# Chunk 3's transposes moved from the crossbar to TensorE, and batch 0's sink rows of v moved up in Pool's queue

## The chip, the cores and the metric

The kernel runs on one core of one Trainium2 chip. Times are device microseconds (us) of an execution; lower is better. The kernel before takes 211.6 us in the median of 6 runs (211.2 to 212.99). The engines are named as in the profile: PE (TensorE, with PEld for its weight loads), DVE (VectorE), ACT (ScalarE), POOL (GpSimd), SP (SyncE, which here only issues transfers).

## What is computed

Attention with a sliding window and four sink positions, followed by a feed-forward layer that takes the maximum of three products:

```python
batch, n_heads, seq, head_dim = (4, 8, 768, 64);  n_sink, window = (4, 128)
n_tokens, d_model, d_ff = (3072, 512, 768)

scores = scale * q @ k.T
keep   = (pos_k < n_sink) | ((0 <= pos_q - pos_k) & (pos_q - pos_k < window))
a      = softmax(where(keep, scores, -1e9))
x      = (a @ v), heads side by side                    # 3072 x 512
h      = maximum(maximum(x @ w1, x @ w2), x @ w3)       # 3072 x 768
out    = h @ w_out                                      # 3072 x 512, float32
```

Inputs and output are float32; products run in bfloat16 with float32 sums.

## The kernel before

The 3072 tokens are cut into 12 chunks of 256, three for each of the four batches. A chunk passes through these steps, each a letter in the order that is written out by hand:

- load (L61): K and Q in halves of four heads (`qk_raw`, four transfers), V in four transfers (`v_raw`), all issued by SP. A gate may be given: a one-element memset on Pool that the load has to wait for.
- cast (L186): to bfloat16, `cast_qk` (L172) four times into `qk_bf` and `cast_v` (L182) twice into `ve`. For chunks 0 and 1 VectorE and Pool share it; from chunk 2 on Pool does it. The layout of `qk_bf` differs by how it will be transposed: by half heads for TensorE, or in one run for the crossbar.
- K and Q (`prep`, L200): four PE transposes each for half the heads into a PSUM tile `pt`; K is then copied by VectorE (two copies, `place_k`, L192) into `kz`, Q by ScalarE (L209) into `qT`. From chunk 2 on `pt` comes from the pool `ps_o`, which has two buffers and also serves the steps A and T.
- D and E: the other way to the same end. `turn` (L215) issues two crossbar transposes on SP, of K to `kT` and of Q straight to `qT`; E (`place_k` from `kT`) copies K with two larger VectorE copies.
- S (`score`, L233): scores of one head, the exponential on ScalarE (L249) and, for each pair of heads, the mask on VectorE (L252).
- Z: sink scores of a chunk (L254), or, for the first chunk of a batch, the gathering of the batch's sink rows of K (`sink_k`, L223).
- A (`av`, L268): products with V for four heads and half the tokens. Chunks other than a batch's first begin with the sink product (L272), which reads `vs`. L280 are the window's products, the first of each head with the earlier block of 128 rows. L285 and L288 normalize.
- T: transposes of the result on PE (L300) and a copy by ScalarE (L301).
- F (L306): one of nine products with w1, w2, w3, taken up by ScalarE (L317) or VectorE (L319). Y (L321): the product with w_out, the copy to `y_sb` (L329), and the stores on SP (L336), issued after the second half.

Work is issued in the order of the program text, and each engine runs its own instructions strictly in that order. Chunks 0, 1 and 2 have an order of their own (L371 to L440), in which small "warm" products fill PE; from L442 on a loop runs ten passes, pass i with the scores and A of chunk i+1, F and Y of chunk i, D and E of chunk i+2 and the load and cast of chunk i+3.

`sink_v(b)` (L163) spreads the four sink rows of V of batch b over the heads: one Pool multiplication (L164) of `vs_raw` with a 0/1 mask `bm`, and a small copy (L168). `vs_raw` holds the sink rows of all batches; SP loads it with four small transfers (L89) between the loads of chunks 0 and 1.

Two places matter for the change. In the opening (L381 to L394) Pool runs: two casts of v of chunk 0, half of chunk 1's K and Q casts, the issue of w1, the other half, the issues of the second and third weights, the gate of load 2, two casts of v of chunk 1, `sink_v(0)`, and zeros for `kz[2]`. And where the opening hands over to the loop (L436 to L440) SP gets, in this order, the stores of chunk 0's output (Y of chunk 0 is in the line before), the two crossbar transposes of chunk 3, load 4, and the stores of chunk 1's output.

Of the kernel before, what the change touches and what calls it, by code (L numbers as in the profile page):

```python
# [16 lines left out]
def kernel(  # L17
# [24 lines left out]
    CPB = S // 256  # L42
# [8 lines left out]
    with tc.manual_schedule():  # L51
# [9 lines left out]
        def load(ci, gate=None):  # L61

            b, c = divmod(ci, CPB)
            t0 = c * 256
            eng = nc.sync
            qk = raw.tile([128, 2, 2, 512], F32, tag="qk_raw", name="qk_raw")
            vr = raw.tile([128, 2, H, D], F32, tag="v_raw", name="v_raw")
            if gate is not None:
                gate.memset(qk[0:1, 0, 0, 0:1], 0.0)
            for g in range(2):  # L70
                for j, src in ((0, k), (1, q)):
                    eng.dma_start(  # L72
                        out=qk[:, j, g].rearrange("p (h i d) -> p h (i d)", h=4, d=D),
                        in_=src[b, 4 * g:4 * g + 4, t0:t0 + 256]
                            .rearrange("h (p i) d -> p h (i d)", i=2))
            for n in range(2):
                for i in range(2):
                    eng.dma_start(  # L78
                        out=vr[64 * i:64 * i + 64, n],
                        in_=v[b, :, t0 + 128 * n:t0 + 128 * n + 128]  # L80
                            .rearrange("h (p i) d -> i p h d", i=2)[i])
            raws[ci] = (qk, vr)
# [17 lines left out]
        def zeros(i, c, eng):  # L100
            for h in range(2):
                eng.memset(kz[CPB * i + c][64 - 64 * h:128 - 64 * h, h], 0.0)
# [37 lines left out]
        def load_w(wi):  # L140
            w = (moe_w1, moe_w2, moe_w3)[wi]
            wt = const.tile([128, DS, d_ff], BF16, name=f"w{wi}")
            nc.gpsimd.dma_start(out=wt, in_=w.rearrange("(a p) f -> p a f", p=128))
            w_sb[wi] = wt
# [18 lines left out]
        def sink_v(b):  # L163
            nc.gpsimd.tensor_tensor(  # L164
                out=vs[0:R, b, :, 0:D],
                in0=vs_raw[:, b].unsqueeze(1).to_broadcast([R, H, D]),
                in1=bm.unsqueeze(2).to_broadcast([R, H, D]), op=ALU.mult)
            nc.gpsimd.tensor_copy(vs[0:R, b, :, D:D + 1], bm.unsqueeze(2))  # L168
# [3 lines left out]
        def cast_qk(ci, j, g, eng):  # L172
            if ci not in bfs:
                bfs[ci] = raw.tile([128, 2, 2, 2, 256], BF16, tag="qk_bf", name="qk_bf")
            src = raws[ci][0][:, j, g].rearrange("p (h i d) -> p h i d", h=4, d=D)
            if ci < CPB:
                dst = bfs[ci][:, j, g]
            else:
                dst = bfs[ci][:, j].rearrange("p i a x -> p i (a x)")[:, :, 256 * g:256 * g + 256]
            eng.tensor_copy(dst.rearrange("p i (h d) -> p h i d", d=D), src)  # L180

        def cast_v(ci, n, eng):  # L182
            b, c = divmod(ci, CPB)
            eng.tensor_copy(ve[b % 2][:, 2 * c + n, :, 0:D], raws[ci][1][:, n])  # L184

        def cast(ci):  # L186
            for j, g in ((0, 0), (1, 0), (0, 1), (1, 1)):
                cast_qk(ci, j, g, nc.gpsimd)
            for n in range(2):
                cast_v(ci, n, nc.gpsimd)  # L190
# [147 lines left out]
        def step(op):  # L338

            name, ci, arg = op[0], int(op[1:3]), op[3:]  # L340
            if ci >= NCH:
                return
            if name in "KQ":
                prep(ci, int(name == "Q"), int(arg))
            elif name == "D":
                turn(ci)
            elif name == "E":
                place_k(ci, kTs.pop(ci), slice(0, NP))
            elif name == "S":
                score(ci, int(arg))  # L350
            elif name == "Z":
                if ci % CPB:
                    sink_score(ci)
                elif ci > 0:
                    sink_k(ci // CPB)
            elif name == "A":
                av(ci, int(arg[0]), int(arg[1]))
            elif name == "T":
                xpose(ci, int(arg))
            elif name == "F":  # L360
                ffn_h(ci, int(arg))
            elif name == "Y":
                ffn_y(ci, int(arg))

        def run(text, **at):
            for tok in text.split():
                c = at[tok[1]]
                step(f"{tok[0]}{c:02d}{tok[2:]}")


        sink_v_init()  # L371
        warm(36)
        cast_qk(0, 0, 0, nc.vector)
        cast_qk(0, 1, 0, nc.vector)
        run("Ka0", a=0)
        warm(4)
# [6 lines left out]
        cast_qk(1, 0, 0, nc.gpsimd)  # L383
        cast_qk(1, 1, 0, nc.gpsimd)
        load_w(0)
        cast_qk(1, 0, 1, nc.gpsimd)
        cast_qk(1, 1, 1, nc.gpsimd)
        load_w(1)
# [1 line left out]
        load(2, nc.gpsimd)  # L390
        cast_v(1, 0, nc.gpsimd)
        cast_v(1, 1, nc.gpsimd)
        sink_v(0)
        zeros(0, 2, nc.gpsimd)  # L394
        run("Sa0 Sa1 Ka1", a=0)
        warm(3)
# [37 lines left out]
        for b in range(1, B):  # L434
            sink_v(b)
        run("Sc3 Sc4 Fb5 Ac00 Sc5 Fb8 Ac01 Sc6 Ya0 Sc7 Ya1", a=0, b=1, c=2)  # L436
        run("Dd", d=3)
        load(4)
        cast(4)
        run("Ac10 Ac11 Yb0 Tc0 Tc1 Yb1 Ed", b=1, c=2, d=3)  # L440

        for i in range(2, NCH):  # L442
            run("Dc", c=i + 2)
# [43 lines left out]
```

## Time and profile before

| | |
|---|---|
| median of 6 runs | 211.6 us |
| the profiled execution | 211.76 us |
| its span, first to last instruction | 210.1 us |
| mean granted PE clock | 0.966 |
| busy: PE, DVE, ACT, POOL | 186.0, 121.2, 107.5, 67.0 us |
| share of the 16 DMA engines taken by SP's queue | 63.5% |

In the slices each digit is the busy share in tenths, over a fortieth of the span. The granted clock is the share of its full speed that PE had. In the chain of waits each step leads back to what released it; in the list by time a line gives start, length, and engine with tile and line. A wait is put down to the instruction that came last before the waiting one could go.

### The profile page before, as it was taken

To read this page: it belongs to the slowest core of one execution; us is meant where nothing else is said; L and a number is where in the kernel's file an instruction comes from. 1 tells how busy PE (TensorE), PEld (TensorE's weight loads), DVE (VectorE), ACT (ScalarE), POOL (GpSimd) and SP (SyncE) were. 2 spreads that over 40 slices of the span, in tenths; PEclk is the share of its full clock that TensorE was granted. 3 is DMA by queue.
4 is the path that set the end of the run, shared out by engine and by line. 5 is a ranking of instruction groups with operands and counts; after the bars stand their busy time and mean duration, and the time that the engine had idled before them with its cause. 6 is when DMAs were issued, how large, how long until landed. Compare 5 with 4: busy or idle time off the path is not lost.

```text
span 210.1 us, 4734 instructions
## 1 busy us (share of the span) xinstructions
PE 186.0 (89%) x1895; PEld 149.1 (71%) x1895; DVE 121.2 (58%) x271; ACT 107.5 (51%) x198; POOL 67.0 (32%) x113
## 2 busy tenths in 40 slices
PE   7765187999929999999999999999999999999991
PEld 7644176887507959969869689599697797796860
DVE  4792042589413875755748837846668477375340
ACT  8865055145433638456465466375472853754321
POOL 7364448997003335340250420701602400000000
PEclk9997579999996999999999999999999999999999
DMA  5999995960199899959939969869579680300304
GB/s 153 230 220 199 214 264 112 258 166 0 38 187 262 172 261 212 256 123 175 265 72 167 295 129 197 208 116 250 139 151 260 135 158 3 87 16 0 100 3 100
DMA packets 75749, 33.37 MB, mean 159 GB/s; under 512 B 45776, under 2 KB 72656, under 8 KB 75728
## 3 DMA queue, kind: packets, MB, share of 16 engines
q1 hardware_dynamic: 73344, 29.93, 63.5%
q0 software_dynamic: 2384, 3.15, 9.0%
q8 instruction: 15, 0.25, 0.5%
q14 instruction: 6, 0.05, 0.1%
HBM read 25.20 MB, written 6.29 MB: 150 GB/s over the span
## 4 chain that ended last, share of the span: by engine, by line
PE 63%; DVE 13%; DMA 8%; SPq 6%; ACT 4%; issue 3%; POOL 1%; DVEq 0%; POOLq 0%
PE h_ps L313 40%; PE y_ps L324 8%; DMA v_raw<-in_v_dram 6%; DVE h_sb L319 5%; PE st L242 4%; DVE x_sb L288 4%; PE o_ps L280 4%; DMA kT<-qk_bf 3%; SPq L78 2%; DVE e_sb L252 2%; ACT e_sb L249 2%; PE st L243 2%; PE xt_ps L300 2%; SPq L72 2%; PE st L240 1%
## 5 line engine op out<-in xcount | busy, mean ns | idle before, releaser
L313 PE MATMUL h_ps<-xT,w 128*128 128x256 bf16 x864 | 109.5, 275 | 0.7 <-ACT xT L301 0.7
L313 PEld LDWEIGHTS <-w 128*128 128x128 bf16 x864 | 82.0, 99 | 10.7 <-issue 0.8
L249 ACT ACTIVATE e_sb<-st 128x512 bf16<-128x512 f32 (+1 forms) x96 | 53.4, 564 | 35.5 <-PE st L243 35.4
L319 DVE TENSOR_TENSOR h_sb<-h_sb,h_ps 128x512 bf16<-128x512 bf16 x72 | 49.2, 684 | 21.4 <-PE h_ps L313 18.9
L180 POOL CAST qk_bf<-qk_raw 128x512 bf16<-128x512 f32 x44 | 29.2, 673 | 85.1 <-DMA qk_raw<-in_k_dram 69.5
L252 DVE TENSOR_TENSOR e_sb<-e_sb,msk 128x1024 bf16<-128x1024 bf16 (+1 forms) x48 | 32.4, 675 | 41.2 <-ACT e_sb L249 41.0
L324 PE MATMUL y_ps<-wo,h_sb 128*128 128x512 bf16 x144 | 35.2, 379 | 0.0
L329 ACT COPY y_sb<-y_ps 128x512 f32<-128x512 f32 x24 | 14.1, 586 | 37.1 <-PE y_ps L324 37.1
L242 PE MATMUL st<-qT,kz 128*128 128x256 bf16 x96 | 26.5, 280 | 5.3 <-DVE kz L196 4.3
L317 ACT CAST h_sb<-h_ps 128x512 bf16<-128x512 f32 x36 | 21.1, 586 | 15.1 <-PE h_ps L313 14.9
L280 PEld LDWEIGHTS <-e_sb 128*128 128x128 bf16 x352 | 17.1, 99 | 8.6 <-issue 5.5
L243 PE MATMUL st<-qT,kz 128*128 128x128 bf16 x96 | 21.4, 224 | 0.0
L288 DVE TENSOR_TENSOR x_sb<-o_ps,rc 128x256 bf16<-128x256 f32 x48 | 20.4, 425 | 1.7
L324 PEld LDWEIGHTS <-h_sb 128*128 128x128 bf16 x144 | 12.4, 98 | 12.5 <-DVE h_sb L319 3.2
L280 PE MATMUL o_ps<-ve,e_sb 128*128 128x65 bf16 x352 | 19.1, 196 | 1.3 <-DVE e_sb L252 1.3
L184 POOL CAST ve<-v_raw 128x512 bf16<-128x512 f32 x24 | 15.7, 662 | 13.0 <-DMA v_raw<-in_v_dram 12.6
L242 PEld LDWEIGHTS <-kz 128*128 128x128 bf16 x96 | 9.5, 99 | 6.8 <-issue 4.5
L240 PE MATMUL st<-qT,kz 128*128 128x128 bf16 x64 | 14.2, 223 | 0.0
L272 PE MATMUL o_ps<-vs,e_sink 128*128 128x260 bf16 x32 | 9.0, 282 | 5.3 <-POOL vs L168 5.3
L301 ACT COPY xT<-xt_ps 128x512 bf16<-128x512 bf16 x24 | 13.2, 595 | 0.7 <-PE xt_ps L300 0.7
L285 DVE RECIPROCAL rc<-o_ps 128x4 f32<-128x4 f32 x48 | 8.4, 176 | 8.4 <-PE o_ps L280 8.4
L196 DVE COPY kz<-kT 64x1024 bf16<-64x1024 bf16 x18 | 9.2, 514 | 5.9 <-DMA kT<-qk_bf 5.6
(44 smaller groups left out, 110.6 us busy)
## 6 DMA issues: line engine op xcount, KB each, us to landing
qk_raw<-in_k_dram SPq DMA_DIRECT2D x24, 256.0 KB, 4.5
qk_raw<-in_q_dram SPq DMA_DIRECT2D x24, 256.0 KB, 5.4
v_raw<-in_v_dram SPq DMA_DIRECT2D x48, 128.0 KB, 4.2
out_dram<-y_sb SPq DMA_DIRECT2D x22, 256.0 KB, 4.3
w<-in_moe_w_dram POOLq DMA_DIRECT2D x3, 768.0 KB, 9.6
wo<-in_moe_w_out_dram POOLq DMA_DIRECT2D x2, 384.0 KB, 5.6
out_dram<-y_sb SPq DMA_DIRECT2D x4, 128.0 KB, 2.3
kT<-qk_bf SPq DMA_TRANSPOSE x9, 5.0
```

The lines of the kernel that those rows point to most:

```text
L180: eng.tensor_copy(dst.rearrange("p i (h d) -> p h i d", d=D), src)
L240: nc.tensor.matmul(st[:, 0], lhsT=kz[(ci - 1) % (2 * CPB)][:, h, p, 128:256], rhs=qh[:, 0], start=True, stop=True)
L242: nc.tensor.matmul(st[:, 1:3], lhsT=kh[:, 0:128], rhs=qh, start=True, stop=True)
L243: nc.tensor.matmul(st[:, 3], lhsT=kh[:, 128:256], rhs=qh[:, 1], start=True, stop=True)
L249: nc.scalar.activation(e[:, h, lo:], st[:, lo:], AF.Exp, scale=scale)
L252: nc.vector.tensor_tensor(out=e[:, :, lo:], in0=e[:, :, lo:], in1=m, op=ALU.mult)
L280: nc.tensor.matmul(o[:, hh], lhsT=es[ci, p][:, h, sl], rhs=ve[b % 2][:, n, 2 * p + h], start=(c == 0 and x == 0), stop=(x == len(blocks) - 1),
L288: nc.vector.tensor_mul(xs[ci, t][:, 4 * g:4 * g + 4], o[:, :, 0:D], rc.unsqueeze(2).to_broadcast([128, 4, D]))
L313: nc.tensor.matmul(hp[:, f], lhsT=w_sb[wi][:, ds, (2 * fp + f) * 128:(2 * fp + f + 1) * 128], rhs=xTs[ci][:, ds, :], start=(ds == 0), stop ...
L317: nc.scalar.copy(dst, hp)
L319: nc.vector.tensor_max(dst, dst, hp)
L324: nc.tensor.matmul(yp, lhsT=hs[ci][:, fb, t * 128:(t + 1) * 128], rhs=wo[:, fb], start=(fb == 0), stop=(fb == FB - 1))
```

## The change

1. Chunk 3 is transposed by PE (K and Q steps), and the crossbar is used from chunk 4 on. `cast_qk` lays chunk 3 out by half heads accordingly. The four `prep` steps stand between the last steps of chunk 2's A, chunk 1's Y and chunk 2's T; D and E of chunk 3 go.
2. `sink_v(0)` goes from behind the v casts of chunk 1 to behind the issue of the first weights, ahead of the second half of chunk 1's K and Q casts.

```diff
@@ cast_qk
-            if ci < CPB:
+            if ci <= CPB:
                 dst = bfs[ci][:, j, g]
             else:
                 dst = bfs[ci][:, j].rearrange("p i a x -> p i (a x)")[:, :, 256 * g:256 * g + 256]
@@ the opening
         cast_qk(1, 0, 0, nc.gpsimd)
         cast_qk(1, 1, 0, nc.gpsimd)
         load_w(0)
+        sink_v(0)
         cast_qk(1, 0, 1, nc.gpsimd)
         cast_qk(1, 1, 1, nc.gpsimd)
         load_w(1)
         load_w(2)
         load(2, nc.gpsimd)
         cast_v(1, 0, nc.gpsimd)
         cast_v(1, 1, nc.gpsimd)
-        sink_v(0)
         zeros(0, 2, nc.gpsimd)
@@ before the loop
         run("Sc3 Sc4 Fb5 Ac00 Sc5 Fb8 Ac01 Sc6 Ya0 Sc7 Ya1", a=0, b=1, c=2)
-        run("Dd", d=3)
         load(4)
         cast(4)
-        run("Ac10 Ac11 Yb0 Tc0 Tc1 Yb1 Ed", b=1, c=2, d=3)
+        run("Ac10 Ac11 Yb0 Tc0 Kd0 Tc1 Qd0 Yb1 Kd1 Qd1", b=1, c=2, d=3)
```

In the text of the order a token is the step's letter, a letter for the chunk, and the step's part: "Kd0" is K of chunk d = 3, first half of the heads.

## The prediction

> **What bounds the kernel now.** I read the 40 slices first, to find stages where TensorE (PE) is not busy; then the waits of PE; then the chain of waits through the two holes; then the busy time by stretches, which gives the clock; last the timeline of each engine around the holes.
>
> The slices, from the page (each is 5.25 us):
>
> ```profile
> PE   7765187999929999999999999999999999999991
> PEclk9997579999996999999999999999999999999999
> ```
>
> From the thirteenth slice on (63 us) PE is full to the end, so nothing after that can be won except by starting it earlier. Two holes lie before: slice five (21 to 26 us) and slice twelve (58 to 63 us), each followed by a low granted clock. The waits put names to them:
>
> ```profile
> PE o_ps L272 <- POOL vs L168: 5.3, 1, 5.3
> PE st L242 <- DVE kz L196: 4.3, 1, 4.3
> ```
>
> The chain, in order of time (start, length, what):
>
> ```profile
> 12.05 11.64 DMA v_raw<-in_v_dram
> ...
> 24.39 1.04 POOL vs L164
> 25.43 0.18 POOL vs L168
> 25.61 0.04 issue
> 25.65 0.38 PE o_ps L272
> ...
> 54.90 0.59 ACT y_sb L329
> ...
> 56.20 0.62 SPq L336
> ...
> 56.91 5.44 DMA kT<-qk_bf
> 62.35 0.02 issue
> 62.38 0.42 DVE kz L196
> 62.83 0.44 DVE kz L196
> 63.26 0.36 PE st L242
> ```
>
> First hole: PE waits for the sink rows, which Pool writes only after the cast of v of chunk 1, whose data land at 23.7. Second hole: chunk 3's crossbar transposes stand in SP's queue behind the stores of chunk 0's output, which wait for the last copy of y (54.90); then comes the transfer. The stretches (length, busy time of PE, PEld, DVE, ACT, POOL, then clock, DMA share, GB/s):
>
> ```profile
> 20.30:25.65 5.35, 0.00 (x1) 0.00 (x1) 0.00 (x0) 0.31 (x1) 1.78 (x3) 0.50 1.15 215
> 25.65:29.00 3.35, 3.35 (x32) 2.79 (x32) 1.82 (x5) 1.19 (x2) 2.29 (x3) 0.55 1.15 226
> 58.90:63.20 4.30, 0.03 (x1) 0.10 (x1) 0.79 (x2) 0.59 (x1) 0.00 (x0) 0.95 1.16 185
> 63.20:66.60 3.40, 3.35 (x19) 2.52 (x19) 0.17 (x2) 1.47 (x3) 1.23 (x2) 0.56 1.11 304
> ```
>
> After each hole PE works some 3.4 us at about half its clock.
>
> **The change part by part.** All times are those of the profiled execution: 211.76 us, of which the span is 210.1 and 1.66 lie around it. It stands 0.16 above the median of 211.6.
>
> *Sink rows of batch 0 earlier.* The pair L164 and L168 goes from behind the second v cast of chunk 1 to behind the issue of w0 (11.97 + 0.93 = 12.90). At the old place it took from 24.43 to 25.61, on the path. What PE waits for at the new order: the first group of Ab00 (the product of chunk 1 that opens the hole) needs the sink rows and the first v cast only (17.70 + 0.62 = 18.32), so it runs as soon as the warm matmuls end, at 20.3. Ab00 and the scores Sb5 behind it, 25.65 to 26.89 in the chain, or 1.24, then lie inside the wait. The second v cast ends at 24.43 and is needed by the second v product of Ab01; the sink product and first v product of Ab01, another 0.25, also go ahead. So the release comes 25.61 - 24.43 = 1.18 earlier and 1.49 less work follows: 2.67. Ab01, Sb6 and Fa0 run at the low clock as before, and the chain then goes by ScalarE (29.28, 29.86) and VectorE (30.39), which take what they took. The low stretch lasts about as long from its new start, so it now reaches into Fa3, which fits in before the mask is ready. I take **2.5**. If Ab00 could not go early, only 1.18 would stay.
>
> What is pushed at the new place: on Pool, the casts of K and Q (second half) of chunk 1, the issues of w1 and w2, the memset that gates load 2. At its shortest the pair costs 1.25 there (1.04 + 0.21); at its longest, by the two slowest rows of the same lines (1.55 at 49.38 and 0.67 at 47.64), 2.22. The K cast (13.08, 0.61) then ends at 14.9 to 15.9. Its transposes begin at 14.85 now, so they come 0 to 1.1 late; but the next step, the Q transposes at 16.29, waits for the Q cast, whose data arrive at 15.25. That cast starts 0 to 0.7 late. What follows it up to 20.3 may shift by as much, and is covered by the 2.5 us that PE still waits for v (from 21.9 to 24.4); without that cover it would cost its 0.7. w1, w2 and chunk 2 move by the same 0.7 at most; w2, the slowest (13.7 us from its issue at 16.92, so 30.6), is first needed about 40, and chunk 2's casts, done at 33.5, at 39.7. The four small sink loads have landed by then: the loads of v behind them on SP reuse their completion counters, and the fourth is issued at 12.05.
>
> A rule speaks against the new place. The row first: a mask on VectorE that takes 0.69 alone took 1.49 at 46.74, while Pool ran L164 (46.65 to 47.69).
>
> The Trainium skill, "SBUF — State Buffer", section "Who interferes with whom", says that a VectorE instruction with two SBUF inputs and a Pool instruction that reads SBUF exclude each other for a whole instruction. By this rule the pair, moved from a stretch where VectorE is idle into one where it is busy, can hold VectorE back by up to one L164, an estimate of 1.0 us, which would make the gain 1.5 if nothing covered it, against 2.5 with the cover that the trace shows.
>
> By the rows the delay is at most 0.8 there, before 16.29, and covered. The three other pairs (46.65 to 51.09) stay where Pool's data put them, while VectorE's work around them comes 2.5 earlier; they may then hit another mask, or none: 0.8 either way, taken as nothing. The first part is 2.5, with ends 0.4 (1.18 - 0.8) and 3.5 (2.67 + 0.8).
>
> *Chunk 3 by TensorE.* Removed: two crossbar transposes on SP (56.91 to 60.63) and the two large kz copies (62.38 to 63.25). Added: 16 PE transposes (8 take 0.61 in L207's row at 42.33, so 0.30 per four), two ScalarE copies of 0.59 (L209), four VectorE copies of 0.42 to 0.44 (L196 from PSUM). They share the two o buffers with Ab's and T's products, so each waits for a copy two steps back. In times of before: Yb0 and Tc0 end at 57.3; Kd0 follows (its buffer is free at 56.78) to 57.6; VectorE copies until 58.5. Tc1 waits for ScalarE's copy of Tc0 (58.25) and ends at 58.6; Qd0 waits for Kd0's copies, ends at 58.95; Yb1 takes 1.3, to 60.25; Kd1 and Qd1 find their buffers free and end at 60.85. Sd0, the first score of chunk 3, has its K (58.5) and Q (59.8) and starts at once, against 63.25: **2.4**. If every copy were waited for in turn (57.3, + 0.3 + 0.87, + 0.3 + 0.59, + 1.3, + 0.3 + 0.87, + 0.3) it would be 62.1 and 1.1; if none were, Yb1's end at 58.77 plus 1.2 gives 60.0 and 3.2. The row nearest is the same pairing at 42.33 to 44.5, where the copies ran beside PE's other work.
>
> *The clock after it.* Two steps of score and FFN take 63.25 to 66.75, or 3.50; the same two at 107.96 take 2.08. With no hole, the 1.42 go. The gaps left in the new stretch are 0.7 us and less. Between 13.80 and 17.20 PE was busy 1.64 of 3.40 at clock 1.00; here it is busy some 2.8 of 3.5. So I take **1.4**; ends 0 (low clock anyway) and 1.8 (the whole pass, 15.30 against 13.50 for its like at 108.3).
>
> *What moves on SP and Pool.* Load 4 no longer stands behind the transposes: 60.68 becomes 56.9, and the hole's 2.5 earlier, 54.4. The stores of chunk 1's output now stand behind it, a store being needed by nobody for two passes. Pool's casts of chunk 4 wait for that load (64.66 to 69.87) and come at about 58.4 to 63.6; chunk 4's transposes, still on SP behind those stores, go at about 61 against 69.57. Their result is wanted 13.2 us after Sd0 (76.48 now), about 70; at 5.0 us to landing it is there by 67. From the next pass on, SP waits for the stores (35.0 us of its waits) as now. So nothing is charged here.
>
> Sum: 2.5 + 2.4 + 1.4 = 6.3. 211.76 - 6.3 = 205.5; by the median 205.3. I say 205.4.
>
> **The rivals.** (a) The prep chain or the clock falls short: the ring makes PE wait for each copy (1.1) and the clock drops (0). For it: two buffers for six users. Against it: the copies are shorter than what PE has to do between. 211.6 - 2.5 - 1.1 = 208.0. (b) The first gain is swallowed before 55 us, by masks that meet Pool's other sink pairs and by the low clock: 0.4 + 2.4 + 1.4 gives 207.4. For it: the 1.49 row; against it: PE is busy 9.67 of the 10 us from 45 to 55, so there is little waiting that could grow. (c) Slower: the stall moves to chunk 4. Its transposes now need the load, Pool's casts and the stores in one row on SP, and load 5 stands behind them. The copies to kz are due at about 70; each us past that delays Sb of the next pass by one. It turns into a loss only if they land after 76.5, some 15 us after their issue at 61, three times the median; then a restart at low clock adds 1.4, so about 213. Against it: before, they landed some 2 us ahead of need with an issue 8 us later.
>
> **How the numbers follow.** This kernel's runs tell about 0.5% (1.1 us) from no change. The likeliest case gets 0.66, (a) 0.13, (b) 0.14, (c) with any unseen loss 0.07. Of (a) and (b) 0.02 reaches within 0.5%, and of (c) 0.02. So faster 0.91, same 0.04, slower 0.05. The likeliest's own range is 204.2 to 206.6; widening it to (a) and (b) gives 203.8 to 208.4, which leaves out the sum of all the small ends on one side.
>
> **What would show it.** The wait of L272 on L168 is gone; a shorter one, about 2.5 us, on the v cast (L184) stands in Ab01 near 24.4. The first score of chunk 3 comes near 58.4, the clock beside it 1.00, eight transposes on SP in place of nine of each kind, and the passes from 73 on are as long as now (14.9 and 13.5). The prediction is wrong if L272 still waits for something near 25, if the clock row after Qd1 shows 0.5 to 0.7, or if a pass shows PE waiting for kT of chunk 4.

## The result and the profile after

The changed kernel takes 204.27 us in the median of 21 runs (202.64 to 209.73), against 211.84 us for the kernel before in the same sets (47 runs). The ratio is 0.9667, 95% interval 0.9637 to 0.9696: faster by 3.3%, or 7.05 us, where 6.3 were forecast. The medians are of all executions; ratios and intervals rest on those within 1.5% of the fastest of each kernel, which in the first set of experiments (the kernel before at 211.35 us) are only its three lowest of eleven, so that the ratios of that set lie above the quotients of the medians.

Single executions of one kernel differ by several us. In the three programs with two traces in the table below, the landing of v of chunk 1 differed by 1.5, 0.5 and 4.5 us, and the span, the same way, by 0.9, 0.5 and 5.5. So single traces are compared below stretch by stretch, and sizes are read from medians and ratios.

The profiled execution took 202.9 us, with a span of 201.2. The slices of the page after:

```profile
PE   7674669999799999999999999999999999999990
PEclk9999999999999999999999999999999999999998
```

The last digit of the clock row apart, no slice is below nine tenths of the clock any more; before, slices four to six and thirteen were. Both nearly empty slices of PE are gone. The waits on PE that remain of the two holes:

```profile
PE o_ps L280 <- POOL ve L184: 1.7, 1, 1.7
```

L272 waits for nothing near 25, and no score waits for a kz copy from the crossbar. The chain in order of time (start, length, what):

```profile
12.85 9.13 DMA v_raw<-in_v_dram
...
22.10 0.82 POOL ve L184
22.92 0.04 issue
22.96 0.37 PE o_ps L280 x7
...
54.61 1.29 PE y_ps L324 x6
55.90 0.45 PE pt L207 x8
56.35 0.11 PE st L242
```

v's second cast is now followed directly by the second product of Ab01, and the crossbar is no longer in this part of the chain: the score of chunk 3 follows the eight transposes Kd1 and Qd1. The stretches (length; busy time of PE, PEld, DVE, ACT, POOL; clock; DMA share; GB/s):

```profile
20.30:21.80 1.50, 0.92 (x15) 0.76 (x15) 0.79 (x4) 1.11 (x2) 0.00 (x0) 1.00 1.16 210
21.80:24.30 2.50, 1.34 (x19) 1.23 (x19) 1.24 (x3) 0.60 (x1) 2.09 (x3) 1.00 1.15 216
52.00:57.00 5.00, 4.29 (x42) 2.94 (x41) 1.97 (x5) 3.21 (x7) 0.61 (x1) 1.00 0.95 252
57.00:60.00 3.00, 3.00 (x31) 2.71 (x29) 1.47 (x4) 2.21 (x6) 1.23 (x2) 1.00 0.92 219
```

PE is busy 2.26 of the 4.00 us of the first two rows, where it stood idle before, and the clock beside it is 1.00, where it was 0.50 and 0.55. In the stretch with the new transposes PE is busy 4.29 of 5.00 us and the clock holds. The passes of the loop after that:

```profile
56.20:69.80 13.60, 13.45 (x137) 10.59 (x135) 10.71 (x26) 7.67 (x16) 5.37 (x8) 1.00 1.00 239
69.80:84.70 14.90, 14.75 (x159) 12.01 (x157) 9.62 (x20) 8.57 (x16) 5.96 (x9) 1.00 0.89 206
84.70:99.60 14.90, 14.75 (x159) 12.00 (x157) 9.26 (x20) 8.57 (x16) 4.18 (x7) 1.00 0.89 177
```

The first pass takes 13.60 instead of 15.30, the two after it the 14.90 that such passes took before.

The two profiled executions differ by 8.9 us of span. Four points in each trace divide that: the start of v's second cast, the start of the long run of F of chunk 1 (Fb0), the first score of chunk 3, and the third score.

| stretch | before | after | difference |
|---|---|---|---|
| start to v's second cast | 23.81 | 22.10 | 1.71 |
| v's second cast to Fb0 | 10.66 | 7.56 | 3.10 |
| Fb0 to the first score of chunk 3 | 28.78 | 26.53 | 2.25 |
| that score to the third | 3.50 | 2.07 | 1.43 |
| the rest of the span | 143.35 | 142.94 | 0.41 |

The first row is when v landed; that it owes anything to the change is not shown (below). The other four make 7.2, close to the 7.05 of the ratio.

### The profile page after: what moved, and what is told of

The parts are those of the page before. It is cut to its first block, busy times and chain, and to the rows that moved or that the text cites. A ratio compares the mean times of both kernels' runs of the same rounds, so it can differ in the third digit from the quotient of the medians.

```text
span 201.2 us, 4768 instructions
## 1 busy us (share of the span) xinstructions
PE 183.4 (91%) x1911; PEld 148.0 (74%) x1911; DVE 122.6 (61%) x273; ACT 108.5 (54%) x200; POOL 67.3 (33%) x113
## 4 chain that ended last, share of the span: by engine, by line
PE 66%; DVE 14%; SPq 6%; ACT 5%; DMA 5%; issue 2%; POOL 0%; DVEq 0%; POOLq 0%
PE h_ps L313 41%; PE y_ps L324 9%; DVE h_sb L319 5%; DMA v_raw<-in_v_dram 5%; DVE x_sb L288 4%; PE st L242 4%; PE o_ps L280 4%; DVE e_sb L252 3%; SPq L78 3%; ACT e_sb L249 3%; PE xt_ps L300 2%; PE st L243 2%; SPq L72 2%; PE sk L258 2%; PE st L240 1%
## 5 line engine op out<-in xcount | busy, mean ns | idle before, releaser
L313 PE MATMUL h_ps<-xT,w 128*128 128x256 bf16 x864 | 107.9, 273 | 0.7 <-ACT xT L301 0.7
L313 PEld LDWEIGHTS <-w 128*128 128x128 bf16 x864 | 81.1, 98 | 9.8 <-issue 0.8
L252 DVE TENSOR_TENSOR e_sb<-e_sb,msk 128x1024 bf16<-128x1024 bf16 (+1 forms) x48 | 31.8, 663 | 38.1 <-ACT e_sb L249 38.0
L242 PE MATMUL st<-qT,kz 128*128 128x256 bf16 x96 | 25.8, 272 | 1.0 <-ACT e_sb L249 0.5
L280 PE MATMUL o_ps<-ve,e_sb 128*128 128x65 bf16 x352 | 18.7, 193 | 3.5 <-POOL ve L184 1.7
L243 PE MATMUL st<-qT,kz 128*128 128x128 bf16 x96 | 20.9, 219 | 0.0
L280 PEld LDWEIGHTS <-e_sb 128*128 128x128 bf16 x352 | 16.6, 98 | 5.2 <-DVE e_sb L252 2.3
L184 POOL CAST ve<-v_raw 128x512 bf16<-128x512 f32 x24 | 16.3, 684 | 9.8 <-DMA v_raw<-in_v_dram 9.0
L240 PE MATMUL st<-qT,kz 128*128 128x128 bf16 x64 | 14.0, 219 | 0.0
L300 PE MATMUL xt_ps<-ident,x_sb 128*128 128x128 bf16 x96 | 9.6, 221 | 4.6 <-DVE x_sb L288 3.2
L300 PEld LDWEIGHTS <-x_sb 128*128 128x128 bf16 x96 | 5.7, 97 | 10.4 <-DVE x_sb L288 9.3
L242 PEld LDWEIGHTS <-kz 128*128 128x128 bf16 x96 | 9.4, 98 | 1.9 <-DVE kz L196 0.2
L243 PEld LDWEIGHTS <-kz 128*128 128x128 bf16 x96 | 9.4, 98 | 1.4 <-issue 1.0
```

Source lines behind the costliest of these rows:

```text
L242: nc.tensor.matmul(st[:, 1:3], lhsT=kh[:, 0:128], rhs=qh, start=True, stop=True)
L243: nc.tensor.matmul(st[:, 3], lhsT=kh[:, 128:256], rhs=qh[:, 1], start=True, stop=True)
L252: nc.vector.tensor_tensor(out=e[:, :, lo:], in0=e[:, :, lo:], in1=m, op=ALU.mult)
L280: nc.tensor.matmul(o[:, hh], lhsT=es[ci, p][:, h, sl], rhs=ve[b % 2][:, n, 2 * p + h], start=(c == 0 and x == 0), stop=(x == len(blocks) - 1),
L300: nc.tensor.transpose(pt[:, ds], x[:, ds * 128:(ds + 1) * 128], ident)
L313: nc.tensor.matmul(hp[:, f], lhsT=w_sb[wi][:, ds, (2 * fp + f) * 128:(2 * fp + f + 1) * 128], rhs=xTs[ci][:, ds, :], start=(ds == 0), stop ...
```

## The experiments

All runs compute the whole output. The same four points, from every trace that is used here:

| kernel | v's second cast starts | to Fb0 | Fb0 to first score of chunk 3 | two steps after it |
|---|---|---|---|---|
| before | 23.81 | 10.66 | 28.78 | 3.50 |
| before, again | 22.29 | 11.02 | 28.38 | 3.74 |
| TensorE part alone | 23.69 | 11.36 | 26.15 | 2.08 |
| before, warm products in the second hole | 23.83 | 10.55 | 29.37 | 2.07 |
| sink part alone | 22.74 | 8.58 | 28.30 | 2.83 |
| sink part alone, again | 27.23 | 8.57 | 28.30 | 4.00 |
| after | 22.10 | 7.56 | 26.53 | 2.07 |
| after, again | 21.65 | 7.37 | 26.44 | 2.07 |
| sink rows between the v casts | 21.04 | 7.37 | 26.54 | 2.07 |
| sink rows twice | 21.27 | 7.97 | 26.52 | 2.08 |
| early crossbar | 20.99 | 7.37 | 25.76 | 2.07 |
| early crossbar, sink rows between | 21.88 | 7.48 | 24.06 | 2.07 |
| the same, weights later | 20.92 | 7.72 | 24.47 | 2.08 |

### The sink part alone

```diff
         load_w(0)
+        sink_v(0)
         ...
         cast_v(1, 1, nc.gpsimd)
-        sink_v(0)
```

> The kernel before with the sink rows of batch 0 moved up alone; chunk 3 stays on the crossbar. By the sum of the prediction it gains 2.5 us (ratio 0.988) and the second hole, 4.3 us with the low clock after it, stands. Rival, from the profile after the change (its first hole was 1.7 us short and the clock beside it 1.00): the short hole no longer lets the clock drop, and the gain is 4 to 5 us (ratio 0.976 to 0.981). Second rival: the early arrival of v in that one profile (21.98 against 23.69) was chance, and the gain is no more than 2.5 in the median.

> The sink rows moved alone, a second time, for the size of this part. From the traces so far the stretch from the second cast of v to the first full F of chunk 1 takes 10.6 to 11.4 us at the old place and 7.4 to 7.6 at the new one with the clock up, 8.6 with it down. So the part is worth 2.3 to 3.4 us (ratio 0.984 to 0.989).

Measured: 207.95 us against 211.35, ratio 0.9876 (0.9719 to 1.0032), which alone settles nothing; the second time 207.04 against 212.32, ratio 0.9784 (0.9706 to 0.9863). So the part is worth some 2.6 to 4.6 us by the two ratios, the first of which does not exclude zero. The forecast 2.5 lies at the lower end, the rival "4 to 5" at the upper. The traces say why both are seen. With the clock up, v's cast to Fb0 takes 7.4 to 8.0, 2.6 to 4.0 less than at the old place (10.55 to 11.36); in the two traces of this part, where PE waited 2.4 and 8.2 us for v and the clock fell, it takes 8.6, or 2.0 to 2.8 less. The second trace is the extreme one, from Pool's timeline (start, length, what, idle before and releaser):

```profile
27.23 0.62 POOL L184 CAST ve<-v_raw 128x512 bf16<-128x512 f32 x1 [9.45 <-DMA v_raw<-in_v_dram]
```

Here v landed at 27.2 with the sink rows long in place; this was an execution of 214.1 us.

### The TensorE part alone

```diff
-            if ci < CPB:
+            if ci <= CPB:
...
-        run("Dd", d=3)
         load(4)
         cast(4)
-        run("Ac10 Ac11 Yb0 Tc0 Tc1 Yb1 Ed", b=1, c=2, d=3)
+        run("Ac10 Ac11 Yb0 Tc0 Kd0 Tc1 Qd0 Yb1 Kd1 Qd1", b=1, c=2, d=3)
```

> The kernel before with chunk 3 transposed by TensorE alone; the sink rows stay behind the casts of v. By the sum of the prediction it gains 2.4 for the hole and 1.4 for the clock, 3.8 us (ratio 0.982), and L272 waits about 5 us for the sink rows as before. If the prep steps wait for each copy and the clock stays low (rival a) it gains 1.1 (ratio 0.995).

> Chunk 3 on TensorE alone, a second time. From the traces so far it takes 2.2 us from the hole and 1.4 from the clock behind it: 3.6 us (ratio 0.983). With the other part this adds up to the 7.0 of the whole change if neither needs the other.

Measured: 208.25 us against 211.35 (no interval), and the second time 207.88 against 212.32, ratio 0.9836 (0.9763 to 0.991), or 3.5 us. The trace of the first keeps the first hole, 6.6 us of waiting of L272, and has 26.15 and 2.08 in the last two columns. Forecast 3.8; rival (a), 1.1, is out. Within these intervals the two parts add up, 3.5 and 2.6 to 4.6 against 7.05, and each is faster alone: neither needs the other. (The trace of the second is not used: its execution took 280.15 us at a mean clock of 0.654.)

### The clock in the second hole by itself

```diff
         run("Ac10 Ac11 Yb0 Tc0 Tc1 Yb1 Ed", b=1, c=2, d=3)
+        warm(70)
```

> The kernel before with 70 warm products (70 x 0.056 = 3.9 us) between chunk 1's last output product and chunk 3's first score, in the second hole; the wait stays, only the clock is held. The prediction's third term says that the low clock after the hole costs 1.4 us: two steps of score and FFN take 2.1 instead of 3.5, and the kernel is 1.4 us faster than before (ratio 0.993). If the clock falls for another reason, nothing changes.

Measured: 209.6 us in the median of 12 runs against 211.48, so 1.9 us, with nothing done but products that nobody reads. The ratio, 0.9752 (0.9671 to 0.9833), shows more than the medians; it rests on two of the twelve (204.25 and 207.1), and I do not take its size. The trace decides: the products in the hole and the first three scores behind it,

```profile
58.67 4.07 PE L111 MATMUL warm<-ident 128*128 128x128 bf16 x70
63.75 0.27 PE L242 MATMUL st<-qT,kz 128*128 128x256 bf16 x1 [1.01 <-DVE kz L196]
...
64.78 0.27 PE L242 MATMUL st<-qT,kz 128*128 128x256 bf16 x1
...
65.82 0.27 PE L242 MATMUL st<-qT,kz 128*128 128x256 bf16 x1
```

The hole is as long as before (first score at 63.75), and yet the two steps take 2.07 in place of 3.50. The third term of the sum, 1.4, is the clock and nothing else.

### Is the place of the sink rows covered

In the changed kernel VectorE's timeline shows what Pool's work did to it. The four small copies of sink K, and the last of the four by itself:

```profile
14.22 1.80 DVE L227 COPY ks<-kz 128x8 bf16<-128x8 bf16 x4
14.86 1.16 DVE L227 COPY ks<-kz 128x8 bf16<-128x8 bf16 x1
```

and Pool's and PE's, beside it:

```profile
13.65 1.07 POOL L164 TENSOR_TENSOR vs<-vs_raw,bm 32x512 bf16<-32x512 f32 x1
14.77 1.20 POOL L180 CAST qk_bf<-qk_raw 128x512 bf16<-128x512 f32 x2
...
16.75 0.28 PE L300 MATMUL xt_ps<-ident,x_sb 128*128 128x128 bf16 x2 [2.06 <-DVE x_sb L288]
```

Before, those copies took 0.51 and PE waited 0.77 there; in all the traces this wait is some 0.25 longer than the copies are. Most of the hold-up is in the last copy, which ran beside the two casts that now come close behind the multiplication; the multiplication itself ended at 14.7, within the first copy. Other traces show less: 0.81 to 1.28 with the sink rows at this place, and 0.41 to 0.86 with the rows elsewhere. Two runs ask whether that matters. One spreads the rows between the two casts of v:

```diff
         load_w(0)
-        sink_v(0)
         ...
         cast_v(1, 0, nc.gpsimd)
+        sink_v(0)
         cast_v(1, 1, nc.gpsimd)
```

> The changed kernel with the sink rows spread between the two casts of v of chunk 1 instead of ahead of chunk 1's second K cast. In the changed kernel the four small copies of L227 took 1.80 us in place of 0.51 beside L164, and the transposes of chunk 0's result waited 2.06. If that is hidden by the wait for v, as the prediction has it, nothing changes (within 0.5 us). If it is on the path, this order is 1 to 1.5 us faster than the changed kernel. If the sink rows come too late there for Ab00 at 20.3, it is up to 1 us slower.

Its VectorE timeline:

```profile
13.99 0.41 DVE L227 COPY ks<-kz 128x8 bf16<-128x8 bf16 x4
```

Measured: 203.43 us against 211.35, ratio 0.972 (0.961 to 0.983). The hold-up is gone and the time is that of the changed kernel (0.9667) within the interval, so 1 to 1.5 us on the path is not seen; the interval, 2.3 us each way, is too wide to exclude 1 us. The other run doubles the suspected cost:

```diff
         load_w(0)
         sink_v(0)
+        sink_v(0)
```

> The changed kernel with the sink rows of batch 0 spread twice at the new place, another 1.25 us of Pool ahead of chunk 1's second K cast, beside VectorE's copies of sink K. By the prediction this place is covered by 2.5 us of waiting for v later on: no change within 0.5 us as long as v lands after about 22. If it is on the path, 1.3 us slower than the changed kernel (204.0). Since v has landed as early as 20.9 in some traces, 0.5 us slower in the median would be a cover that is thinner than I took it for.

Measured: 203.54 us against 212.32, ratio 0.9667 (0.959 to 0.9744), the ratio of the changed kernel to four digits. The interval, 1.6 us each way, does not exclude the 1.3 us that the path would show. In its trace the copies take 1.95, v's second cast starts at 21.27, and nothing on PE waits for L168. But nothing waits for v any more either: the first product of Ab00 starts at 21.82, where it was 20.33 in the changed kernel, and v's second cast to Fb0 takes 7.97 instead of 7.56 and 7.37. So twice the cost uses up the cover, and in this trace, where the clock was at 0.50 from 17.6 to 21.0 as well, about half a us comes through. In both traces of the changed kernel itself PE waits 1.75 and 2.2 us for v behind these copies, so there the place is covered; where v lands at 21 or before, as in three traces of other orders (waits of 0.2 to 0.4), next to no cover is left.

### Was it the crossbar, or its place in the queue

```diff
+        run("Dd", d=3)
         run("Sc3 Sc4 Fb5 Ac00 Sc5 Fb8 Ac01 Sc6 Ya0 Sc7 Ya1", a=0, b=1, c=2)
-        run("Dd", d=3)
```

The sink part is as in the changed kernel; chunk 3 stays on the crossbar, but its transposes are issued before the stores of chunk 0's output.

> The sink rows moved up; chunk 3 stays on the crossbar, but its two transposes are issued ahead of the stores of chunk 0's output, once Pool has cast chunk 3. If the hole came from the place in SP's queue and not from the crossbar, the hole closes: the first score of chunk 3 follows Yb1 directly, 2.1 us earlier than with the 16 transposes on TensorE (58.77 against 60.85 in the prediction's times), so some 2 us faster than the changed kernel (ratio about 0.957 to the kernel before). If the crossbar is slow by itself at that place (5.4 us from issue, next to load 3 and Pool's work), the hole shrinks but stays and it is 0 to 2 us slower than the changed kernel.

Measured: 202.23 us against 211.35, ratio 0.9658 (0.953 to 0.9786). SP's queue and the end of the stage, from the timeline:

```profile
45.27 1.33 SPq L219 DMA_TRANSPOSE kT<-qk_bf  x1
...
46.70 1.24 SPq L219 DMA_TRANSPOSE qT<-qk_bf  x1
...
50.20 1.33 SPq L336 DMA_DIRECT2D out_dram<-y_sb  x2
...
52.03 0.87 DVE L196 COPY kz<-kT 64x1024 bf16<-64x1024 bf16 x2
...
52.82 1.46 PE L324 MATMUL y_ps<-wo,h_sb 128*128 128x512 bf16 x6
...
54.12 0.27 PE L242 MATMUL st<-qT,kz 128*128 128x256 bf16 x1
```

The hole is closed by the crossbar as well: the copies to kz are done before Yb1 ends, and the first score follows it at once. So the hole came from the stores that stood ahead of the transposes, not from the crossbar. From Fb0 to the first score it takes 25.76, 0.7 less than with TensorE and not 2.1: in this trace two masks in the stretch were held up, and L280 waited 1.13 and 0.81 for them, against 0.75 in the changed kernel.

With the sink rows between the casts of v as well (both edits above):

> Sink rows between the two casts of v, and chunk 3's crossbar transposes issued ahead of the stores of chunk 0's output. If the 2.1 us of prep work on TensorE and ScalarE are all on the path, it is about 2 us faster than the changed kernel and equal to the run with the early crossbar and the first place of the sink rows; if the sink rows at their new place cost something too, another 0.5 to 1 us faster.

Measured: 203.24 us against 211.48, ratio 0.959 (0.9517 to 0.9662); Fb0 to the first score 24.06, 2.4 less than the changed kernel. The changed kernel in the same set:

> The changed kernel, unchanged, for a second trace and for times on the chip of the others of this set. If the landing of v is chance, the wait in Ab01 is another than 1.75 us (0.4 to 3); 7 us faster than before (ratio 0.967) in the median.

It took 203.96 us, ratio 0.9678 (0.9618 to 0.9738). The intervals overlap: the point estimates put the early crossbar 0.9% ahead, about the 2 us expected, but it is not shown apart.

### When v lands

> The kernel before, unchanged, for a second trace. In the profiles so far the second half of chunk 1's v landed at 23.7 and 23.6 where the sink rows stood behind the casts, and at 20.9, 20.9, 22.0 and 22.6 where they stood ahead. If that time is chance from run to run, it lies anywhere between 20.9 and 24 here; if the old order itself makes it late, it is 23.5 or more again.

Measured: 210.93 us, and v's second cast at 22.29, well below 23.5. Over all traces it starts at 22.3 to 23.8 with the old order and at 20.9 to 27.2 with the new places. The two overlap, and the same program had 22.7 and 27.2, so the order alone does not set it. But eight of the nine traces with a new place lie between 20.9 and 22.74, where the four of the old order begin at 22.29, so that the order has no part in it is not shown either; the 1.7 us of the first row of the table stay open. Whether the other weights that are under way keep it back is the last question:

```diff
-        load_w(1)
-        load_w(2)
         load(2, nc.gpsimd)
         cast_v(1, 0, nc.gpsimd)
         sink_v(0)
         cast_v(1, 1, nc.gpsimd)
+        load_w(1)
+        load_w(2)
```

(on the order with the early crossbar and the sink rows between the casts)

> The order with the early crossbar and the sink rows between the casts of v, and the issues of the second and third weights moved behind both casts of v. In all traces the second half of v lands at 20.9 to 23.8, some 8 to 11 us after its issue, while those two weights (768 KB each) are under way. If they are what keeps v, it lands at 19 to 20, the wait in Ab01 is gone, and this is 1 to 2 us faster than the same order without the move (203.2 us). If the weights are then late themselves (needed at about 30 and 35, issued at about 20), up to 1.5 us of it comes back as a wait of F for w. If v is kept by w0 or the load before it, nothing changes.

Measured: 201.32 us against 212.32, ratio 0.954 (0.9477 to 0.9603), the lowest ratio of all. In the trace v's second cast starts at 20.92, hardly before the earliest without the move (20.99), so "lands at 19 to 20" is a miss; PE waits 0.2 us for it and F waits for no weight. Five of its six runs lie between 200.55 and 202.0. Whether the move or the two edits under it make that, the runs do not settle: its interval overlaps that of the order without it (0.9517 to 0.9662). Against the changed kernel the intervals, 0.9477 to 0.9603 and 0.9637 to 0.9696, each to the kernel before in its own sets, do not touch: this order is faster than both kernels.

## Why the prediction was right

The sign, the range (203.8 to 208.4 for 204.27) and the mechanism held. The sum, 6.3, was 0.75 us short of the 7.05 of the ratio, and the time said, 205.4, was 1.1 above the median. The terms are off by this much.

- **First hole, 2.5 forecast, 3.1 measured in the pair of profiles.** The order was read rightly: Ab00 and Sb5 ran into the wait (L272 at 20.33, as "at 20.3"), and the wait that remains is on L184, 1.75 us in one trace and 2.2 in the other. The step that failed is "Ab01, Sb6 and Fa0 run at the low clock as before". In both traces the clock stays at 1.00 through this wait, and the stretch from v's cast to Fb0 shrinks by 3.1 instead of 2.5 in the pair. That is in part luck: by the last section the clock stayed up narrowly. In the trace before it had been at 0.50 from 18.4, ahead of the hole, so that the fall was not the hole's doing, as the prediction read it. In the two traces where the wait was 2.4 us or more the clock fell and the part was worth 2.0 to 2.8.
- **What is pushed.** VectorE's delay, "at most 0.8", was mis-sized: in the pair the copies of sink K took 1.29 longer and PE's wait at L300 grew by as much. The price was taken from a mask beside one multiplication and did not count the casts that come close behind it on Pool. That it is covered held in both traces of the changed kernel, with 1.75 and 2.2 us to spare; the doubled run shows that there is not much more. The Trainium skill, "SBUF — State Buffer", section "Who interferes with whom", holds that VectorE copies in a mode that uses both ports and Pool's instructions exclude each other for a whole instruction; these rows agree in kind, with 1.80 against 0.51, but that the copies ran in such a mode no run here shows. The gain of 1.5 that the prediction works out for the case without cover did not come about.
- **Masks against Pool's other sink pairs, taken as nothing.** One met a mask again: 1.29 at 49.44, and PE waited 0.75 for it, where before the mask at 46.74 took 1.49 and PE then waited 0.33 for the next one. Rival (b), that this swallows the gain, is out.
- **Second hole, 2.4 forecast, 2.25 measured** (28.78 to 26.53). Of the waits listed, the one for ScalarE's copy of Tc0 is there with 0.71, as forecast; the rest of the prep ran as laid out.
- **Clock after it, 1.4 forecast, 1.43 measured**, and shown alone by the warm products. The row that it leaned on, 1.64 of 3.40 us busy at clock 1.00, was near the edge: 1.2 us after it the clock fell.
- **What moves on SP and Pool.** Load 4 was issued at 51.81 and chunk 4's transposes at 60.58 (about 61 forecast); the kz copies began at 68.00 straight behind the other work of VectorE, without a wait for kT. Rival (c) had no part in it.

## What to carry to other kernels

Look for what a wait keeps idle behind it: moving a small instruction out from behind a late transfer won not only its own 1.2 us but the work that could then run inside the wait and, in these traces, a clock that stayed up. A transfer that is late may be late because of what stands ahead of it in its queue; here, issuing the same crossbar transposes before the stores closed the hole as well as moving them to TensorE did, without TensorE's extra work.

## What the runs showed of the hardware

The same small transfer (the second half of v of chunk 1, its loads issued at 10 to 14 us) landed between 20.9 and 27.2 us over the traces, and at 22.7 and 27.2 in two executions of one program. What makes it vary was not found.

How long a single wait of PE is does not tell whether the clock falls: it stayed at 1.00 through waits of 1.75 and 2.2 us for v and fell after one of 2.4 us; but with the sink rows twice and with the early crossbar it fell at 17.6 and 16.3, after waits at L300 of 2.2 and 1.1 us, and in the changed kernel one of 2.06 there left it up. The traces show another order. Within a trace the changes of the clock lie whole multiples of 3.41 us apart (before: at 18.41, 28.65, 62.79 and 66.20). Stretches on this raster, with PE's busy time, the clock, the DMA share and GB/s, two from before and two from after:

```profile
15.00:18.41 3.41, 1.52 (x23) 1.00 1.02 171
18.41:21.83 3.42, 1.89 (x12) 0.50 1.17 213
15.50:18.91 3.41, 1.62 (x24) 1.00 1.10 186
18.91:22.33 3.42, 1.96 (x26) 1.00 1.15 206
```

In the thirteen traces of the table the clock fell thirteen times ahead of the kernel's end, each time after such a stretch with PE busy 0 to 1.65 us; the lowest after which it stayed up are the 1.62 shown and 1.76. It rose again after stretches with 2.8 us or more. The raster lies elsewhere in each execution, so whether a wait of some 2 us costs the clock is in part chance. The second hole, 3.6 to 4.3 us long, cost it in each of the four traces that kept it without the warm products.

K's crossbar transpose took SP 1.33 to 1.34 us in the three traces in which SP had issued nothing for 1.0 to 1.5 us before it. Elsewhere, issued 0.1 us behind another transfer, it took 1.5 to 2.6, mostly 2.3. Q's took 1.24 as a rule in both. That the pause is the reason is not shown.
